# Whole-array products in the second routing's search, and fewer and earlier products of ones around the overflow loop

## The chip, the cores and the metric

The kernel runs on one core of one Trainium2 chip. The metric is the device time of one execution in microseconds (us). The engines are named as in the profile: PE is TensorE, PEld its weight loads, DVE is VectorE, ACT is ScalarE, POOL is GpSimd and SP is SyncE, which here only starts transfers.

## The reference, cut to what matters

Three steps follow each other: a causal retention attention, a first mixture of experts that routes each token to its best expert, and a second one that hands out places greedily, with a capacity of 576 tokens for each of 8 experts.

```python
x = attn(q, k, v)                       # 8 batches, 8 heads, 576 positions, 64 wide -> x [4608, 512]
skip = x @ w_skip; e1 = argmax(x @ w_gate)           # first mixture: where skip > 0
x[do] = x[do] + gate * relu(x[do] @ w1[e1]) @ w2[e1]
logits = x @ w_gate2                                 # second mixture
for idx in argsort(-logits.flatten()):               # best (token, expert) pair first
    tok, e = idx // 8, idx % 8
    if assigned[tok] < 0 and counts[e] < 576:
        assigned[tok] = e; counts[e] += 1
out[assigned == e] = relu(x[assigned == e] @ w1b[e]) @ w2b[e]
```

## The kernel before, in words

Everything is unrolled into one instruction stream per engine. The order on each engine is the order in which the Python code issues it; where the search of the second routing is woven into the matrix products, the functions `tick` and `task` decide it from counted columns, without a look at any measured time.

**Stages.** Attention runs over 36 tiles of 128 tokens. The first routing makes lists of token numbers. Then `over_blocks` (L895) opens a loop on the device that handles tokens over an expert's first 352 places; its count `nov` is computed on the chip, and all engines meet at its entrance and at its exit. Eight experts of the first mixture follow, then eight of the second. An expert's work is `layer1` (products `l1p`, L658, three passes of 128x128 weights in split fp32) and `layer2` (products `l2p`, L689), both on PE.

**The search.** The second routing needs, expert by expert, the score at which the 576th place falls. `phase(i)` (L1157) finds it by a search with base 32 in `ITS = 5` iterations; seven of the eight phases search, which makes 35 iterations. One iteration is a chain between DVE and PE:

- DVE makes the masks `M` (L179 from `digits`), PE counts with ten products into `cnt` (L1189, 128x128 weights in bf16, 32 columns moving), DVE copies to `part` in fp16 (L1191);
- PE adds up four interleaved parts into `sum` (L1195): four products whose weights are 32 columns of the identity, `eye4[:, a]`, every fourth column of `eye`, in fp16, so that the output has 32 rows; 8 columns move. DVE compares to `fl` (33 rows, the last a constant);
- PE adds the 33 rows of `fl` with a product of ones into `nfl` (L1199: weights of 33 rows and 128 columns, 8 columns moving), DVE takes the maximum (`nfs`).

Between these small products stand the large ones of `layer1` and `layer2`. After the five iterations the list of the expert's tokens is made: `idp` (L1270), then `idq` (L1279), sixteen products with 32 columns of the same `eye`, each quarter of the outputs at its own 32 columns of the array. Once a phase, the product `cct` (L1302) adds counts over all 128 rows: ones of 128x128, 8 columns moving, bf16.

**Products of ones.** `warm` (L220) issues products of ones with ones whose result nobody reads. 70 stand behind the first routing and ahead of the overflow loop (L598); ten stand behind each of the three sets of transposes `trp` (L639, called `turn`) that bring the first expert's gathered tokens into layout behind the loop (L1051). ACT copies a transposed tile to `xTH`, DVE writes the rest to `xTL`; `layer1` starts with `xTH` and needs `xTL` for its second product. Between these, the generator `gws` puts the gate weights (`gw`, `MV`) on DVE.

Of the kernel before, what the change touches and what calls it, by code (L numbers as in the profile page):

```python
# [11 lines left out]
BF16 = mybir.dt.bfloat16  # L12
F16 = mybir.dt.float16
# [8 lines left out]
N, DM, FF, E = 4608, 512, 1024, 8  # L22
NT = 36
P = 128
# [19 lines left out]
K = 32  # L44
# [118 lines left out]
def block_kernel(ctx, tc, q_c, k_c, k_r, v_r, wg, wg2, w1a, w2a, w2t, w1b, w2b, cst, dtab, out, dbg=None):  # L163
    nc = tc.nc
    V = nc.vector
# [3 lines left out]
    const = ctx.enter_context(tc.tile_pool(name="const", bufs=1))  # L169
# [8 lines left out]
    def tt(o, x, y, op):  # L178
        V.tensor_tensor(o, x, y, op)  # L179

    def ts(o, x, s1, op0, s2=None, op1=None):
        if op1 is None:
            V.tensor_scalar(o, x, s1, None, op0)
        else:
            V.tensor_scalar(o, x, s1, s2, op0, op1)

    def stt(o, x, sc, y, op0, op1):
        V.scalar_tensor_tensor(o, x, sc, y, op0, op1)  # L188

    def red(o, x, op):  # L190
        V.tensor_reduce(o, x, AX.X, op)
# [3 lines left out]
    def rt(name, shape, dt=F32, tag=None):  # L195
        return (rp if rp2[0] is None or tag else rp2[0]).tile(shape, dt, name=name, tag=tag or name)

    def last(x, n):
        return x.unsqueeze(2).to_broadcast([P, x.shape[1], n])

    def mid(x, n):
        return x.unsqueeze(1).to_broadcast([P, n, x.shape[1]])
# [4 lines left out]
    ones = const.tile([P, P], BF16, name="ones")  # L207
    iota2 = const.tile([P, P, 2], BF16, name="iota2")
    uv = const.tile([P, 2, NQ], BF16, name="uv")
    eye = const.tile([P, P], F16, name="eye")  # L210
    eye4 = eye.rearrange("p (k q) -> p q k", q=4)
    LG = const.tile([P, NT, 17], F32, name="LG")
    ident = cs[:, C_ID:C_ID + P]
    iota = cs[:, C_IOTA:C_IOTA + P]
# [5 lines left out]
    def warm(pool, tag, n):  # L220
        p = pool.tile([P, 512], F32, name="idle", tag=tag)
        for _ in range(n):
            nc.tensor.matmul(p[:, 0:P], lhsT=ones, rhs=ones, start=True, stop=True)
# [143 lines left out]
    with ExitStack() as actx:  # L367
# [4 lines left out]
        ps_x = actx.enter_context(tc.tile_pool(name="ps_x", bufs=1, space=PSUM))  # L372
# [136 lines left out]
        def tables():  # L509
            tt(um1, cs[:, C_MASK:C_MASK + P], ident, ALU.subtract)  # L510
            tt(um1, um1, ones, ALU.subtract)
            V.tensor_copy(eye, ident)
            V.tensor_copy(iota2, last(iota, 2))
            V.memset(uv, 0.0)
            V.tensor_copy(uv[:, 0, 0:NT], u_t)
            V.tensor_copy(uv[:, 1, 0:NT], v_t)
            none = rawp.tile([P, DM], F32, name="none", tag="wraw")
            nc.gpsimd.memset(none, 0.0)
            nc.gpsimd.dma_start(X[N:N + TRASH, :], none)
            nc.gpsimd.dma_start(LT[N:N + TRASH, :], none[:, 0:E])  # L520
# [29 lines left out]
        for i in range(-4, NT):  # L550
            if i in (-1, 1, 2, 3):
                c = max(i, 0) + 1
# [42 lines left out]
        route_ids()  # L595
        for _ in fuse:
            pass
        warm(ps_x, "xr", 70)  # L598

    if "LG" in dbg:  # L600
        nc.sync.dma_start(dbg["LG"], LG)
# [6 lines left out]
    ps1 = ctx.enter_context(tc.tile_pool(name="ps1", bufs=3, reuse_waits="tile", space=PSUM))  # L608
# [352 lines left out]
    kq = rt("kq", [P, K, 4], BF16)  # L961
    hl = rt("hl", [P, 2, NQ], BF16)
    z = rt("z", [P, NQ])
    fl = rt("fl", [K + 1, E], BF16)
    zb = rt("zb", [P, NQ], BF16)
    MQ = [None]

# [13 lines left out]
    def claims(a, b, src):  # L981
        n = b - a
        c = rt("c1", [P, NC, E])[:, a:b]
        red(val[:, a:b], src, ALU.max)
        tt(c, src, last(val[:, a:b], E), ALU.is_equal)
        yield
        tt(c, c, mid(w8, n), ALU.mult)
        red(mx2[:, a:b], c, ALU.max)
        yield
        stt(mx2[:, a:b], mx2[:, a:b], 1.0, un[:, a:b], ALU.add, ALU.mult)  # L990
        ts(mx2[:, a:b], mx2[:, a:b], -1.0, ALU.add)
        tt(OH[:, a:b], c, last(mx2[:, a:b], E), ALU.is_equal)
# [5 lines left out]
    def first_claims():  # L998
        V.memset(pen, 0.0)
        V.memset(vq[:, NC:NQ], 0.0)  # L1000
        V.memset(OH[:, NC:NQ], 0.0)
        V.memset(hl, 0.0)
        V.memset(fl[K:K + 1], -float(ZOFF))
        ts(kq, last(iota[:, 0:K], 4), 1.0 - ZOFF, ALU.add)
        V.tensor_copy(rm, rem)
        yield
        for _ in claims(0, NT, L2[:, 0:NT, :]):
            yield
        yield
        L2f = L2[:, 0:NT, :].rearrange("p t e -> p (t e)")  # L1010
        red(ext[:, 0:1], L2f, ALU.max)
        red(ext[:, 1:2], L2f, ALU.min)
        ts(ext[:, 1:2], ext[:, 1:2], -1.0, ALU.mult)
# [33 lines left out]
    t0 = turns(0, T1, (2,))  # L1047
    for n, j in enumerate(t0):
        next(gws)
        j()  # L1050
        warm(ps1, "l1", 10)  # L1051
    next(gws)
    for j in gathers_a(1):
        j()
# [102 lines left out]
    def phase(i):  # L1157
# [7 lines left out]
        if i < E - 1:  # L1165
            if i:
                ts(pen, opn, BIG, ALU.mult, -BIG, ALU.add)
                Lm = rt("Lm", [P, NC, E], tag="rk")
                tt(Lm, L2, mid(pen, NC), ALU.add)
                tt(rm, rem, pen, ALU.subtract)  # L1170
                yield 0.7
                for _ in claims(0, NC, Lm):
                    yield 0.7
                yield 0.7
            part = rt("part", [P, 4, E], F16)
            nf1 = rt("nf1", [P, 1])
            cnd = rt("cnd", [P, 1])
            for it in range(ITS):
                if it == 0:
                    masks(vq, lo0, inv0)  # L1180
                else:
                    masks(z, nf, ZMUL)
                while rest:
                    rest.pop(0)()
                yield MASK + LAG

                p = psm.tile([P, 4, E], F32, name="cnt", tag="sm")
                for t in range(NG):
                    nc.tensor.matmul(p.rearrange("p a e -> p (a e)"), lhsT=MQ[0][:, t].rearrange("p k a -> p (k a)"),  # L1189
                                     rhs=OH[:, 4 * t:4 * t + 4, :].rearrange("p a e -> p (a e)"), start=(t == 0), stop=(t == NG - 1))  # L1190
                V.tensor_copy(part, p)  # L1191
                yield 0.3 + LAG
                p = psm.tile([P, E], F32, name="sum", tag="sm")
                for a in range(4):
                    nc.tensor.matmul(p[0:K, :], lhsT=eye4[:, a], rhs=part[:, a, :], start=(a == 0), stop=(a == 3))  # L1195
                tt(fl[0:K], p[0:K, :], rm[0:K], ALU.is_ge)
                yield 0.3 + LAG
                p = psm.tile([P, E], F32, name="nfl", tag="sm")
                nc.tensor.matmul(p, lhsT=ones[0:K + 1, :], rhs=fl, start=True, stop=True)  # L1199
                nf = nfs[:, it:it + 1]  # L1200
                red(nf, p, ALU.max)
            ts(es, p, nf, ALU.is_equal)
            ts(nf1, nf, 1.0, ALU.add)
            tt(es, es, w8, ALU.mult)
            red(mc, es, ALU.max)
            ts(eix[:, i:i + 1], mc, -1.0, ALU.mult, 8.0, ALU.add)
            yield "expert"
            gl = rt("gl", [P, NC], BF16)
            gh = rt("gh", [P, NC], BF16)
            eo = rt("eo", [P, NC], BF16)  # L1210
            ge = rt("ge", [P, NC], BF16)
            ts(gl, zb[:, 0:NC], nf, ALU.is_ge)
            ts(gh, zb[:, 0:NC], nf1, ALU.is_ge)
            ts(eo, mx2, mc, ALU.is_equal)
            tt(ge, gh, eo, ALU.mult)
            tt(gl, gl, eo, ALU.mult)
            tt(sb[:, 1], gl, ge, ALU.subtract)
            stt(sb[:, 0], asg, mc, ge, ALU.is_equal, ALU.add)
            yield 1.8 + LAG
        else:  # L1220
            tt(es, opn, w8, ALU.mult)
            red(mc, es, ALU.max)
            ts(eix[:, i:i + 1], mc, -1.0, ALU.mult, 8.0, ALU.add)
            yield "expert"
            stt(sb[:, 0], asg, mc, un, ALU.is_equal, ALU.add)
            V.memset(sb[:, 1], 0.0)
            yield 0.5 + LAG
        p = psm.tile([P, 2, 2 * NC], F32, name="pfx", tag="sm")
# [22 lines left out]
        h1, l1 = hl[:, 0], hl[:, 1]  # L1251
# [16 lines left out]
        p = psm.tile([P, 2, 20, 4], F32, name="idp", tag="sm")  # L1268
        for t in range(NG):
            nc.tensor.matmul(p.rearrange("p j h q -> p j (h q)"), lhsT=OHl[:, t].rearrange("p k q -> p (k q)"),  # L1270
                             rhs=MV2[:, :, t].rearrange("p j h q -> p j (h q)"), start=(t == 0), stop=(t == NG - 1))
        pt2 = rt("pt2", [P, 2, 20, 4], F16)
# [3 lines left out]
        p = psm.tile([P, 10], F32, name="idq", tag="sm")  # L1276
        for a in range(4):
            for q in range(4):
                nc.tensor.matmul(p[32 * a:32 * a + 32, :], lhsT=eye4[:, q], rhs=pt2.rearrange("p j (c a) q -> p a q j c", a=4)[:, a, q],  # L1279
                                 start=(q == 0), stop=(q == 3), tile_position=(0, 32 * a), skip_group_check=True)  # L1280
        iv = rt("iv", [P, 5])
        ts(iv, p[:, 5:10], -1.0, ALU.add)
# [2 lines left out]
        if i < E - 1:  # L1285
# [15 lines left out]
            p = psm.tile([P, E], F32, name="cct", tag="sm")  # L1301
# [189 lines left out]
```

## Time and profile before

| | |
|---|---|
| median of 3 runs | 993.41 us (990.68, 993.41, 996.14) |
| the profiled execution | 988.81 us, span of the trace 987.0 us |
| busy in the span | PE 934.9 us, DVE 651.8, ACT 321.8, POOL 236.5 |
[...]

The profiled execution is one of its own, 4.6 us (0.5%) below the median of the three runs. The span runs from the first to the last instruction. A busy PE is not a PE at its peak, since products are pipelined: what one costs is read from the starts of those around it.

### The profile page before, as it was taken

What the parts mean: (1) busy time and instruction counts of PE and PEld (TensorE: products, weight loads), DVE (VectorE), ACT (ScalarE), POOL (GpSimd) and SP (SyncE); (2) the same over time, 40 slices, a digit from 0 to 9 for tenths busy, and PEclk for the clock granted to TensorE, in tenths of its full rate; (3) what the DMA queues carried; (4) which work ended last, traced back from release to release, by engine and by line L of the source; (5) the groups of instructions that cost most, each with busy time, mean ns of one, the idle gap of its engine ahead of it and who ended that gap; (6) DMA issues with size and microseconds to landing.
All of it is one profiled execution on the core that took longest, in us unless ns stands there. A gap on an engine that the chain in (4) does not pass through costs nothing.

```text
span 987.0 us, 20836 instructions
## 1 busy us (share of the span) xinstructions
PE 934.9 (95%) x8382; PEld 780.0 (79%) x8382; DVE 651.8 (66%) x1674; ACT 321.8 (33%) x610; POOL 236.5 (24%) x208
## 2 busy tenths in 40 slices
PE   7999998799999999999799999999999999999997
PEld 6788876788888888885587796887968869788886
DVE  3466585479999999865776668566685666744230
ACT  1233333134334433430143233332333323334320
POOL 2322231213544433223201203113031030330101
PEclk9999999999999999999789999999999999999999
DMA  9999994454446445410424306033060240632301
GB/s 324 361 389 361 346 376 161 153 213 157 146 168 210 134 161 176 152 53 30 149 89 154 114 22 224 23 116 141 23 224 33 100 157 12 220 117 92 107 6 43
DMA packets 57684, 153.96 MB, mean 156 GB/s; under 512 B 8464, under 2 KB 9232, under 8 KB 57328
## 3 DMA queue, kind: packets, MB, share of 16 engines
q1 hardware_dynamic: 40608, 107.50, 31.0%
q0 software_dynamic: 10496, 30.93, 9.1%
q10 hardware_dynamic: 6480, 14.16, 3.9%
q8 instruction: 67, 1.10, 0.4%
q14 instruction: 33, 0.27, 0.1%
HBM read 127.43 MB, written 25.13 MB: 155 GB/s over the span
## 4 chain that ended last, share of the span: by engine, by line
PE 67%; DVE 22%; DMA 5%; issue 4%; ACT 1%; SPq 1%; POOL 0%; POOLq 0%; ACTq 0%; DVEq 0%
PE l1p L658 28%; PE l2p L689 19%; DVE junk L756 5%; PE xTp L444 3%; PE l2p L712 3%; DVE w1L L179 3%; PE sc L418 3%; DVE w2L L179 2%; PE trp L639 2%; PE xrp L472 2%; DVE xTL L179 2%; PE xTp L441 1%; PE Sp L456 1%; DMA qT<-in_q_c_dram 1%; DMA vR<-in_v_r_dram 1%
## 5 line engine op out<-in xcount | busy, mean ns | idle before, releaser
L658 PE MATMUL l1p<-xTH,w1H 128*128 128x288 f32 (+1 forms) x768 | 243.3, 317 | 3.2 <-DVE hL L188 2.6
L658 PE MATMUL l1p<-xTL,w1H 128*128 128x288 f32 (+1 forms) x768 | 235.3, 306 | 2.0 <-DVE xTL L179 1.8
L658 PE MATMUL l1p<-xTH,w1L 128*128 128x288 f32 (+1 forms) x768 | 234.3, 305 | 0.0
L689 PE MATMUL l2p<-w2H,hH 128*128 128x512 f32 (+1 forms) x448 | 185.9, 415 | 0.0
L689 PE MATMUL l2p<-w2H,hL 128*128 128x512 f32 (+1 forms) x448 | 175.8, 392 | 0.0
L689 PE MATMUL l2p<-w2L,hH 128*128 128x512 f32 (+1 forms) x448 | 175.1, 391 | 0.0
L658 PEld LDWEIGHTS l1p<-xTH,w1H 128*128 128x128 f32 x768 | 145.4, 189 | 8.3 <-DVE hL L188 5.4
L658 PEld LDWEIGHTS l1p<-xTL,w1H 128*128 128x128 f32 x768 | 145.5, 189 | 3.4 <-DVE xTL L179 3.0
L658 PEld LDWEIGHTS l1p<-xTH,w1L 128*128 128x128 f32 x768 | 145.5, 189 | 0.0
L188 DVE SCALAR_TENSOR_TENSOR hL<-l1p,hH 128x288 fp32r<-128x288 f32 (+1 forms) x192 | 85.7, 453 | 86.6 <-ACT hH L667 84.0
L667 ACT ACTIVATE hH<-l1p 128x288 fp32r<-128x288 f32 (+1 forms) x192 | 78.5, 410 | 180.3 <-PE l1p L658 174.9
L718 POOL DMA_INDIRECT out_dram<-y,ids x40 | 43.7, 1092 | 389.4 <-DVE y L179 226.7
L689 PEld LDWEIGHTS l2p<-w2H,hH 128*128 128x128 f32 (+1 forms) x448 | 82.5, 184 | 24.2 <-issue 8.3
L756 DVE SCALAR_TENSOR_TENSOR junk<-x,wgb 128x512 f32<-128x512 f32 (+1 forms) x144 | 99.0, 688 | 3.1
L689 PEld LDWEIGHTS l2p<-w2H,hL 128*128 128x128 f32 (+1 forms) x448 | 82.4, 184 | 20.5
L689 PEld LDWEIGHTS l2p<-w2L,hH 128*128 128x128 f32 (+1 forms) x448 | 82.8, 185 | 15.0
L619 POOL DMA_INDIRECT xg<-X,ids x64 | 79.6, 1244 | 57.3 <-issue 22.9
L640 ACT ACTIVATE xTH<-trp 128x512 fp32r<-128x512 f32 (+2 forms) x64 | 35.6, 558 | 119.0 <-PE trp L639 103.4
L244 ACT ACTIVATE w1H<-wraw 128x1024 fp32r<-128x1024 f32 x64 | 65.2, 1053 | 24.4 <-DMA wraw<-in_w1b_dram 20.6
L179 DVE TENSOR_TENSOR w1L<-wraw,w1H 128x1024 fp32r<-128x1024 f32 x60 | 71.4, 1220 | 2.3 <-ACT w1H L244 1.8
L179 DVE TENSOR_TENSOR w2L<-wraw,w2H 128x1024 fp32r<-128x1024 f32 x60 | 72.7, 1213 | 0.0
L244 ACT ACTIVATE w2H<-wraw 128x1024 fp32r<-128x1024 f32 x64 | 67.4, 1054 | 15.8 <-PE l2p L689 7.3
(255 smaller groups left out, 1143.1 us busy)
## 6 DMA issues: line engine op xcount, KB each, us to landing
wraw<-in_w2a_dram SPq DMA_DIRECT2D x31, 512.0 KB
wraw<-in_w1b_dram SPq DMA_DIRECT2D x30, 512.0 KB, 3.3
wraw<-in_w2b_dram SPq DMA_DIRECT2D x30, 512.0 KB
wraw<-in_w1a_dram SPq DMA_DIRECT2D x28, 512.0 KB, 4.9
kT<-in_k_c_dram SPq DMA_DIRECT2D x36, 256.0 KB, 4.8
qT<-in_q_c_dram SPq DMA_DIRECT2D x36, 256.0 KB, 6.1
vR<-in_v_r_dram SPq DMA_DIRECT2D x36, 256.0 KB, 5.2
X<-xo ACTq DMA_DIRECT2D x36, 256.0 KB, 5.2
```

Of the source, the lines that this page charges most:

```text
L179: V.tensor_tensor(o, x, y, op)
L188: V.scalar_tensor_tensor(o, x, sc, y, op0, op1)
L244: nc.scalar.activation(h, r, AF.Copy)
L418: nc.tensor.matmul(sc[hh][c, pr, 64 * kh:P], lhsT=d["k"][r, pr, c], rhs=d["q"][r, pr, 64 * kh:P], start=True, stop=True, tile_position=(64 ...
L444: nc.tensor.matmul(xTp[o, hh, x:x + P], lhsT=d["vs"][:, 2 * pr + hh, :], rhs=d["ret"][:, hh, pr, :], start=(c == 0), stop=True, skip_group ...
L619: nc.gpsimd.indirect_dma_start(out=t[0:n, :], out_offset=None, in_=X[:, :], in_offset=bass.IndirectOffsetOnAxis(ap=ids[0:n, :], axis=0))
L640: nc.scalar.activation(h[:, :, off:off + n], p[:, :, 0:n], AF.Copy)
L658: nc.tensor.matmul(o, lhsT=wx[:, c:c + P], rhs=xx[:, k, a:b], start=(n == 0), stop=(n == 11))
L667: nc.scalar.activation(hh[0][:, f, a:b], o, AF.Relu)
L689: nc.tensor.matmul(p[0:n, :], lhsT=x[:, f, off:off + n], rhs=y[:, c:c + 512], start=(f == 0 and j == 0), stop=(f == 7 and j == 2))
L718: nc.gpsimd.indirect_dma_start(out=dst[:, :], out_offset=bass.IndirectOffsetOnAxis(ap=idx, axis=0), in_=src[0:n, :], in_offset=None)
L756: V.scalar_tensor_tensor(j[0:n], x2[0:n], 1.0, wgb[e // 4][0:n, e % 4], ALU.mult, ALU.mult, accum_out=dst[0:n, e:e + 1])
```

## The change

Three parts. (1) `strip` takes the place of `eye`: for each of the four interleaved parts, a tile of 128x128 in fp16 whose first 32 columns are those columns of the identity and whose others are zero. The four products of `sum` use all 128 columns and write all 128 rows, of which DVE still reads 32. `idq` still uses 32 columns, now adjacent ones. (2) `fl` has 128 rows, zero from row 33 on (set once in `first_claims`), and `nfl` uses ones of 128x128. (3) The products of ones ahead of the overflow loop go from 70 to 16; behind it, 16, 4 and 4 stand ahead of the three sets of transposes, where ten stood behind each.

```diff
-    eye = const.tile([P, P], F16, name="eye")
-    eye4 = eye.rearrange("p (k q) -> p q k", q=4)
+    strip = const.tile([P, 4, P], F16, name="strip")
@@ tables()
-            V.tensor_copy(eye, ident)
+            V.memset(strip, 0.0)
+            V.tensor_copy(strip[:, :, 0:32], ident.rearrange("p (k q) -> p q k", q=4))
@@ behind the first routing
-        warm(ps_x, "xr", 70)
+        warm(ps_x, "xr", 16)
@@ first_claims()
-    fl = rt("fl", [K + 1, E], BF16)
+    fl = rt("fl", [P, E], BF16)
+        V.memset(fl, 0.0)
         V.memset(fl[K:K + 1], -float(ZOFF))
@@ behind the overflow loop
     for n, j in enumerate(t0):
         next(gws)
+        warm(ps1, "l1", 16 if n == 0 else 4)
         j()
-        warm(ps1, "l1", 10)
@@ phase()
-                    nc.tensor.matmul(p[0:K, :], lhsT=eye4[:, a], rhs=part[:, a, :], start=(a == 0), stop=(a == 3))
+                    nc.tensor.matmul(p, lhsT=strip[:, a, :], rhs=part[:, a, :], start=(a == 0), stop=(a == 3))
                 tt(fl[0:K], p[0:K, :], rm[0:K], ALU.is_ge)
...
-                nc.tensor.matmul(p, lhsT=ones[0:K + 1, :], rhs=fl, start=True, stop=True)
+                nc.tensor.matmul(p, lhsT=ones, rhs=fl, start=True, stop=True)
@@ the list
-                nc.tensor.matmul(p[32 * a:32 * a + 32, :], lhsT=eye4[:, q], rhs=pt2..., ...
+                nc.tensor.matmul(p[32 * a:32 * a + 32, :], lhsT=strip[:, q, 0:32], rhs=pt2..., ...
```

PE's order inside a search iteration, between two products of layer two, before the change:

```order
L689 MATMUL l2p<-w2H_5910,hL 128x512
L1195 LDWEIGHTS eye
L1195 MATMUL sum<-part,eye 32x8
...
L689 MATMUL l2p<-w2H_5910,hH 128x512
L689 MATMUL l2p<-w2L_5911,hH 128x512
L689 MATMUL l2p<-w2H_5910,hL 128x512
L1199 LDWEIGHTS ones
L1199 MATMUL nfl<-fl,ones 128x8
```

And with the change (the lines of the changed kernel are two or three higher):

```order
L691 MATMUL l2p<-w2H_5851,hL 128x512
L1198 LDWEIGHTS strip
L1198 MATMUL sum<-part,strip 128x8
...
L691 MATMUL l2p<-w2H_5851,hH 128x512
L691 MATMUL l2p<-w2L_5852,hH 128x512
L691 MATMUL l2p<-w2H_5851,hL 128x512
L1202 LDWEIGHTS ones
L1202 MATMUL nfl<-fl,ones 128x8
```

Nothing moved here: the same number of products stands at the same places, and only the output's rows and the weights' names differ. PE's order at the exit of the overflow loop (L897 before), before the change, from the loop's branch to the first product of layer one:

```order
L897 UNCONDITIONAL_BRANCH
L639 MATMUL trp<-cs,xg 128x128 x4
L223 LDWEIGHTS ones
L223 MATMUL idle<-ones 128x128
...
L639 MATMUL trp<-cs,xg 128x96 x4
L223 LDWEIGHTS ones
L223 MATMUL idle<-ones 128x128
...
L658 MATMUL l1p<-xTH,w1H_956 128x352
```

And with the change:

```order
L899 UNCONDITIONAL_BRANCH
L224 LDWEIGHTS ones
L224 MATMUL idle<-ones 128x128
...
L641 MATMUL trp<-cs,xg 128x128 x4
L224 LDWEIGHTS ones
L224 MATMUL idle<-ones 128x128
...
L641 MATMUL trp<-cs,xg 128x96 x4
L660 MATMUL l1p<-xTH,w1H_957 128x352
```

The first set of transposes, which was PE's first work behind the loop, now has sixteen products of ones ahead of it, and none stand between the last set and layer one. On DVE, ACT, POOL and SP the order is that of before, but for DVE's two memsets.

## Rows read from the trace of the kernel before

**Rows 1.** The page's chain that ended last, by engine.

```profile
PE 67%; DVE 22%; DMA 5%; issue 4%; ACT 1%; SPq 1%; POOL 0%; POOLq 0%; ACTq 0%; DVEq 0%
```

**Rows 2.** The chain around one expert's search: start us, us, what.

```profile
599.86 0.18 DVE iv L183
...
614.99 0.61 DVE xTL L179
...
617.68 0.22 PE sum L1195 x4
...
622.95 0.26 PE cnt L1189 x10
```

**Rows 3.** PE's tile sum, all of the run: duration ns min/median/max, starts.

```profile
L1195 PE MATMUL sum<-part,eye x140: 167/174/195, 449.7 to 835.0; 128*32 128x8 f16 x140
```

**Rows 4.** PE in order of time around one nfl and one sum: start us, us.

```profile
619.49 0.40 PE L689 MATMUL l2p<-w2H,hL 128*128 128x512 f32 x1
619.81 0.18 PE L1199 MATMUL nfl<-fl,ones 33*128 33x8 bf16 x1
619.92 0.51 PE L689 MATMUL l2p<-w2H,hH 128*128 128x512 f32 x1
620.26 0.40 PE L689 MATMUL l2p<-w2L,hH 128*128 128x512 f32 x1
620.50 0.40 PE L689 MATMUL l2p<-w2H,hL 128*128 128x512 f32 x1
...
624.27 0.39 PE L689 MATMUL l2p<-w2H,hL 128*128 128x512 f32 x1
624.59 0.29 PE L1195 MATMUL sum<-part,eye 128*32 128x8 f16 x4
624.81 0.50 PE L689 MATMUL l2p<-w2H,hH 128*128 128x512 f32 x1
625.14 0.40 PE L689 MATMUL l2p<-w2L,hH 128*128 128x512 f32 x1
```

**Rows 5.** PE in order of time around one cct.

```profile
603.70 0.39 PE L689 MATMUL l2p<-w2H,hL 128*128 128x512 f32 x1
603.93 0.18 PE L1302 MATMUL cct<-ccb,ones 128*128 128x8 bf16 x1
603.97 0.48 PE L689 MATMUL l2p<-w2H,hH 128*128 128x512 f32 x1
604.29 0.39 PE L689 MATMUL l2p<-w2L,hH 128*128 128x512 f32 x1
```

**Rows 6.** The chain at the overflow loop: start us, us, what.

```profile
176.15 4.05 DMA xg<-X,ids
```

**Rows 7.** PE around the overflow loop, with idle time before a row and its releaser.

```profile
177.85 0.89 PE L223 MATMUL idle<-ones 128*128 128x128 bf16 x13 [0.52 <-issue]
181.76 1.11 PE L639 MATMUL trp<-cs,xg 128*128 128x128 f32 x4 [3.02 <-issue]
182.67 1.27 PE L223 MATMUL idle<-ones 128*128 128x128 bf16 x10
183.73 1.06 PE L639 MATMUL trp<-cs,xg 128*128 128x128 f32 x4
...
188.21 0.43 PE L658 MATMUL l1p<-xTL,w1H 128*128 128x352 f32 x1 [0.85 <-DVE xTL L179]
```

**Rows 8.** DVE behind the overflow loop, in order of time.

```profile
183.54 0.69 DVE L179 TENSOR_TENSOR xTL<-trp,xTH 128x512 fp32r<-128x512 f32 x1 [1.53 <-ACT xTH L640]
...
187.60 0.55 DVE L179 TENSOR_TENSOR xTL<-trp,xTH 128x384 fp32r<-128x384 f32 x1
```

**Rows 9.** By stretch: us, busy (instructions) of PE, PEld, DVE, ACT, POOL, then PEclk, DMA.

```profile
182.00:184.00 2.00, 2.00 (x16) 1.93 (x16) 0.47 (x2) 1.04 (x2) 1.63 (x2) 0.50 0.21 37
```

**Rows 10.** DVE in the attention, where the constants are made.

```profile
36.76 0.29 DVE L513 CAST iota<-cs 128x256 bf16<-128x256 f32 x1
```

**Rows 11.** The chain in the same stretch.

```profile
36.75 5.95 DMA vR<-in_v_r_dram
```

More of the change, by code (lines that the diff above doesn't have):

```diff
@@ L1278, in phase @@
             for q in range(4):
-                nc.tensor.matmul(p[32 * a:32 * a + 32, :], lhsT=eye4[:, q], rhs=pt2.rearrange("p j (c a) q -> p a q j c", a=4)[:, a, q],
+                nc.tensor.matmul(p[32 * a:32 * a + 32, :], lhsT=strip[:, q, 0:32], rhs=pt2.rearrange("p j (c a) q -> p a q j c", a=4)[:, a, q],
                                  start=(q == 0), stop=(q == 3), tile_position=(0, 32 * a), skip_group_check=True)
```

## Prediction

> **What bounds the kernel now.** I read the chain that ended last first: two thirds of the span are PE and 22% DVE [rows 1]. A cost on PE therefore counts only where the chain runs over PE, so the next view is the chain around one expert's search [rows 2]. It goes over DVE from the first operation on `idq`'s result (599.86) to the split of a transposed tile that ends at 615.60, and from there over PE: `sum` stands in it at 617.68 and `cnt` of the next iteration at 622.95. Walking the whole chain I find 35 `sum` and 35 `nfl`, which is every iteration of every phase; the 140 products of `sum` [rows 3] are four for each. The stretch of DVE work starts from PE's last product on the list, so time saved ahead of it lets it start earlier. Nothing in the search waits for DVE in these rows: PE is the limit there.
>
> Third I read PE in order of time. What a small product costs the large ones is not its own duration (those overlap) but the shift of the starts around it: from the start of the last large product ahead to the start of the second large product behind, less two normal steps. One step is 0.23 (603.70 to the next product's start; 620.26 to 620.50 is 0.24 after rounding) [rows 4, 5], so 0.46 for two; it is the same in all three cases below, and cancels where I subtract them.
>
> - `nfl`, 33 rows: 619.49 to 620.26 is 0.77, less 0.46: **0.31 us** [rows 4]. It starts 0.32 behind the product ahead, 0.09 late; the next follows 0.11 behind it and the one after that 0.34.
> - `sum`, four products with 32 columns: 624.27 to 625.14 is 0.87, less 0.46: **0.41 us** [rows 4]. The start is again 0.09 late, the four take 0.22, the step behind is 0.33, 0.10 too long.
> - `cct`, all rows and columns, and otherwise what `nfl` is to become (ones of 128x128, 8 columns moving, bf16): 603.70 to 604.29 is 0.59, less 0.46: **0.13 us** [rows 5]. It starts after exactly one step, and the next product follows 0.04 behind it; only the step of 0.32 after that is too long, by 0.09.
>
> So a product that uses a part of the array starts late by 0.09 and lets the next one start 0.07 later than a whole one does. What stays with the whole one is the 0.09 behind it.
>
> [...]
>
> **The change, part by part.**
>
> *`nfl` on the whole array.* The operation becomes `cct`'s: 0.31 - 0.13 = 0.18 saved, 35 times: **-6.3 us**. This is the safest term, since the same form stands in the trace. The rows of `fl` that it adds are zeros and already in place; the memset that puts them there is one of 128x8, below the 0.29 of a cast of 128x256 [rows 10], once, and I take it as nothing.
>
> *`sum` on the whole array.* No row has fp16 weights of 128 columns. The nearest is `cnt`: ten whole-array products in bf16 in 0.26 [rows 2]; with 0.04 for the first [rows 5] each further one takes (0.26 - 0.04) / 9 = 0.024. Four then cost 0.13 + 3 x 0.024 = 0.20 against 0.41 now: 0.21 saved, 35 times: **-7.35 us**. The bound on the other side comes from the only fp16 loads there are, those of `sum` itself: each further product takes (0.22 - 0.11) / 3 = 0.037 with 32 columns [rows 4]. If that is a load's time and grows with the columns, a product takes 4 x 0.037 = 0.147, and four cost 0.13 - 0.024 + 4 x 0.147 = 0.69: 0.28 lost each time, +9.8 us. I take `cnt`'s price, because it is a two-byte type with the same number of columns and rows on the same engine among the same neighbours; the type's letter is the only difference.
>
> [...]
>
> *`idq`.* Still 32 columns, adjacent now instead of every fourth. I take nothing. If its sixteen products went from 0.037 to 0.024 each, eight lists would save 1.7 us; that goes into the lower bound.
>
> *The constants.* DVE gets a memset of 128x512 in fp16, and the cast reads by strides. The cast of 128x256 next to it takes 0.29 [rows 10]; once or twice that, while the chain stands for 5.95 us on an attention load [rows 11]. The load hides it; without that cover it would cost 0.3 to 0.6 us.
>
> *Fewer products ahead of the overflow loop.* All engines wait at the loop for the third gather, which lands at 176.15 + 4.05 = 180.20 [rows 6]. PE's last product of ones ends at 177.85 + 0.89 = 178.74 [rows 7], so it was 1.5 us early and 54 products fewer bring nothing: 0. [...]
>
> *Sixteen products ahead of the first transposes.* PE is the last engine out of the loop, and its first work there was the transposes at 181.76 [rows 7]. They decide `xTH`, and DVE starts on `xTL` at 183.54 after 1.53 us of idling for it [rows 8]. From there DVE works without a break to 187.60 + 0.55 = 188.15 (three `xTL` with the gate weights between them), and layer one's second product starts at 188.21, released by the last `xTL` [rows 7, 8]. So what delays the first transposes delays layer one by as much. Ten products of ones took 183.73 - 182.67 = 1.06 at half clock [rows 7, 9]; sixteen take **+1.7 us**. [...] The products taken away between and behind the transposes saved nothing before, since DVE was the limit there; they give nothing back. Queued behind the sixteen on PE are the transposes alone, and ACT, DVE and then PE itself wait for those.
>
> **The sum.** -6.3 - 7.35 + 1.7 = -11.95, say -12.0 us. Against the profiled execution that is 988.8 - 12.0 = 976.8. That execution lies 4.6 us below the median of the three runs; the mean of the four shown is 992.3, and 992.3 - 12.0 gives **980.3 us**, which I state. A change of this kernel under 0.5%, 5 us, can hardly be told from none.
>
> **The rivals.**
>
> 1. *Fp16 loads grow with their columns* (the other side). Place: the four loads of `strip`, 35 times. The sum is -6.3 + 9.8 + 1.7 = +5.2, or **997.5**. It decides against the change where a further product takes over 0.11: there four cost 0.106 + 4 x 0.11 = 0.54, 0.13 more than now, which eats -6.3 + 1.7. For it: no fp16 load of this width in the trace. Against it: `cnt`. Chance 4%. [...]
> 2. *They grow by half as much.* Halfway between 0.024 and 0.147 is 0.085; four cost 0.106 + 4 x 0.085 = 0.45, 0.04 more than now, +1.3 in all. The sum is -6.3 + 1.3 + 1.7 = -3.3, **989**: no change that can be told. Chance 4%.
> 3. *DVE takes over in the search.* Each iteration is a ring of DVE and PE; PE's part loses 0.39. If DVE's other work (splits of weights of over 1 us in its queue) holds up half of the iterations, half the gain goes: -6.8 + 1.7 = -5.1, **987**. For it: DVE is 22% of the chain [rows 1] and owns the stretch from 599.86 to 615.60 [rows 2]. Against it: no iteration's `sum` waits for DVE there now. Chance 8%.
> 4. *The clock stays low into layer one.* With no products of ones behind the last transposes, PE idles longer ahead of layer one; if that keeps the 0.50 of rows 9 for 2 to 4 us of layer one, 1 to 2 us more: **982**. It changes the size alone. Chance 15%.
> 5. *The loop ends earlier.* If PE's arrival and not the gather had decided, 54 products at 0.89 / 13 = 0.068 would bring up to -3.7: **976.6**. Against it: 178.74 lies ahead of 180.20 [rows 6, 7]. Chance 5%.
>
> **How the numbers follow.** The main case has 64%, and with rivals 4 and 5, which only shift it, 84%. All of these are faster by over 0.5%; rival 3 stands at the edge and is split. Faster 0.88, within 0.5% 0.08, slower 0.04. For the range, the lowest value is the profiled execution with `idq`'s 1.7 or part of rival 5 taken off: 975. The highest is the median of the three runs less rival 3's 5.1: 988. Rivals 1 and 2 stay outside.
>
> **What would show it.** In the changed profile `sum` and `nfl` start one step behind the product ahead, with no 0.09; `nfl` reads like `cct`, 0.13; `sum` has 0.10 to 0.12 from its first start to the next large product, where 0.45 or more would be rival 1. From 449 to 835 us, the stretch of the 35 iterations, some 13 us are gone. Behind the loop the first transposes start 1.7 us after PE's first product of ones, at a granted clock of 0.50, and layer one's second product starts 1.7 us later against the landing of the third gather. The prediction is wrong if DVE rows appear as releasers of `sum` or `cnt` that had none, or if DVE's stretch after the list grows by what PE saved.

## The result, and the profile after

The changed kernel took 980.28 us (median of 4 runs, 978.94 to 981.93); the kernel before, timed beside it, took 992.04 (median of 4, 990.19 to 996.14). The ratio is 0.9877 with a 95% interval of 0.9838 to 0.9915: 8 to 16 us faster. 980.3 was forecast.

The profiled execution took 981.48 us; its span of 979.6 is 7.4 us shorter than that of before. That is less than the medians say, so I first ask where in the span the difference lies. The table cuts the span at events that both traces have: the last transpose of the attention (`xrp`), the first product of the eighth expert of the first mixture (the search begins in that expert's work), and the first product of the lists (`idq`) of the third and of the seventh searching phase. The last stretch holds 20 of the 35 iterations, the one ahead of it 15. Behind the seventh list the two kernels take the same time (136.7 and 136.6 us).

| us | to the last xrp | to the eighth expert | to the third list | to the seventh list |
|---|---|---|---|---|
| before | 165.55 | 254.04 | 179.83 | 250.95 |
| changed kernel | 167.46 | 258.85 | 173.48 | 243.22 |
| difference | +1.91 | **+4.81** | **-6.35** | **-7.73** |

The attention, which the change leaves alone, differs by 1.9 us between the two executions; over the profiles shown here its end lies anywhere from 164.2 to 172.7. Behind it two things are to be read: the search gives 7.73 for 20 iterations, 0.387 each (35 x 0.387 = 13.5), and something between attention and search takes 4.81. The 7.73 is read from the first products of the two lists, before and after:

```profile
599.42 0.34 PE L1279 MATMUL idq<-pt,eye 128*32 128x10 f16 x16
850.37 0.34 PE L1279 MATMUL idq<-pt,eye 128*32 128x10 f16 x16
```

```profile
599.79 0.31 PE L1282 MATMUL idq<-pt,strip 128*32 128x10 f16 x16
843.01 0.31 PE L1282 MATMUL idq<-pt,strip 128*32 128x10 f16 x16
```

**The search.** The page's chain by engine of the changed kernel; PE had 67% before and DVE 22% [rows 1]:

```profile
PE 64%; DVE 23%; DMA 6%; issue 5%; ACT 1%; POOL 0%; SPq 0%; POOLq 0%; ACTq 0%; DVEq 0%
```

The chain around the same expert's search in the changed kernel (start us, us, what), against [rows 2]:

```profile
600.19 0.18 DVE iv L183
...
615.31 0.61 DVE xTL L179
615.96 0.66 PE trp L641 x4
...
618.01 0.10 PE sum L1198 x4
...
622.97 0.26 PE cnt L1192 x10
```

The order is that of before, `sum` still stands in the chain as work of PE, and has 0.10 there where it had 0.22. DVE's stretch behind the list lasts from 600.19 to 615.92, 15.73; before it was 15.74. Over the whole run PE idles for the masks `M` ahead of `cnt` 4.8 us in six places and for `part` ahead of `sum` 0.9 us in one, the same in both kernels. PE in order of time in the changed kernel (start us, us, product, rows*columns of the weights, moving tile):

```profile
619.68 0.40 PE L691 MATMUL l2p<-w2H,hL 128*128 128x512 f32 x1
619.92 0.18 PE L1202 MATMUL nfl<-fl,ones 128*128 128x8 bf16 x1
619.96 0.47 PE L691 MATMUL l2p<-w2H,hH 128*128 128x512 f32 x1
620.27 0.39 PE L691 MATMUL l2p<-w2L,hH 128*128 128x512 f32 x1
...
624.29 0.39 PE L691 MATMUL l2p<-w2H,hL 128*128 128x512 f32 x1
624.52 0.26 PE L1198 MATMUL sum<-part,strip 128*128 128x8 f16 x4
624.64 0.48 PE L691 MATMUL l2p<-w2H,hH 128*128 128x512 f32 x1
624.96 0.39 PE L691 MATMUL l2p<-w2L,hH 128*128 128x512 f32 x1
```

`nfl` starts 0.24 behind the product ahead, which is one step, without an idle time, and the next large one 0.04 behind it: 619.68 to 620.27 is 0.59, less two steps of 0.23 is 0.13, where [rows 4] gave 0.31. `sum` starts 0.23 behind the product ahead, the next follows 0.12 later, and 624.29 to 624.96 less 0.46 is 0.21, where it was 0.41. The median over all iterations among large products is 0.12 to 0.13 for `nfl` and 0.20 to 0.21 for `sum`. A further fp16 product takes (0.114 - 0.039) / 3 = 0.025 us, with the same medians' time from `sum`'s and from `nfl`'s start to the next large product.

All 140 products of `sum` now have 128 columns. The tile in the changed kernel, against [rows 3] (duration ns min/median/max, starts): a product's own duration is hardly changed, and would have told nothing.

```profile
L1198 PE MATMUL sum<-part,strip x140: 166/166/180, 456.3 to 828.0; 128*128 128x8 f16 x140
```

**Behind the overflow loop.** The chain of the changed kernel there, against [rows 6]:

```profile
178.05 4.75 DMA xg<-X,ids
```

And PE in order of time in the changed kernel, with the idle time ahead of a row and its releaser, against [rows 7]:

```profile
184.31 1.89 PE L224 MATMUL idle<-ones 128*128 128x128 bf16 x16 [7.91 <-issue]
185.99 1.06 PE L641 MATMUL trp<-cs,xg 128*128 128x128 f32 x4
...
188.23 0.50 PE L641 MATMUL trp<-cs,xg 96*128 96x96 f32 x4
189.55 0.43 PE L660 MATMUL l1p<-xTH,w1H 128*128 128x352 f32 x1 [0.82 <-ACT xTH L642]
192.33 0.66 PE L660 MATMUL l1p<-xTL,w1H 128*128 128x352 f32 x1 [2.35 <-DVE xTL L179]
192.79 0.49 PE L660 MATMUL l1p<-xTH,w1L 128*128 128x352 f32 x1
193.08 0.49 PE L660 MATMUL l1p<-xTH,w1H 128*128 128x352 f32 x1
```

The gather lands at 182.80 and PE's first product behind the loop starts at 184.31, 1.51 later; before it was 180.20 and 181.76, 1.56 later. So the gather still sets the end of the loop. But it took 4.75 where it took 4.05, and PE's first product out of the loop starts 16.85 behind the attention's last transpose, where it started 16.21 behind. That is no chance of two executions: from the last transpose to PE's exit it is 16.85 to 17.25 in all six profiles with 16 products of ones ahead of the loop, and 16.14 to 16.53 in all eight with 70. Of the edits only the 54 products fewer stand ahead of this landing in just those six; why the gather takes longer, no run tells. The first transposes start 1.68 behind the first product of ones. Layer one's second product starts 8.02 behind PE's first product out of the loop, where it was 188.21 - 181.76 = 6.45. Its idle time ahead is 2.35, where it was 0.85, and the products behind it follow each other at 0.29. The windows of the changed kernel show why (us; busy time and instructions of PE, PEld, DVE, ACT, POOL; PEclk; DMA share; GB/s):

```profile
184.00:188.00 4.00, 3.69 (x28) 3.63 (x29) 0.74 (x2) 1.04 (x2) 2.71 (x3) 0.51 0.32 80
188.00:191.00 3.00, 1.16 (x11) 0.72 (x8) 2.86 (x9) 1.09 (x2) 0.12 (x1) 1.00 0.72 199
191.50:198.00 6.50, 5.67 (x19) 5.67 (x20) 2.10 (x6) 0.46 (x1) 0.00 (x0) 0.50 0.21 74
```

The granted clock (PEclk, a share of the full one) was 0.51 from 184 to 188, the ones and transposes, 1.00 from 188 to 191, where PE was busy for 1.16 us, and 0.50 again from 191.5 to 198. In the second profile of the changed kernel (`after_again`, below) it was 0.50 from 184 to 188 and 0.54 from 192 to 198, and layer one's first product, at 190.53, lasted 0.66 where it lasted 0.43 in the first profile. In the kernel before the same products followed each other at 0.16, and the clock was 1.00:

```profile
188.30:195.00 6.70, 6.70 (x70) 6.57 (x71) 2.29 (x7) 0.93 (x2) 0.00 (x0) 1.00 0.39 144
```

Layer one of the first expert has 96 products. From the start of its second to that of its last it took 16.46 us before and 19.07 now (this is what "the 96 products took" means below): **2.6 us** lost at the lower clock. With 8.02 - 6.45 = 1.57 that is 4.2 of the 4.81 between attention and search; the 0.64 by which PE leaves the loop later is the rest.

### The profile page after: what moved, and what is told of

It reads as the page before. It is cut to its first block, busy times and chain, and to the rows that moved or that the text cites. A ratio compares the mean times of both kernels' runs of the same rounds, so it can differ in the third digit from the quotient of the medians.

```text
span 979.6 us, 20718 instructions
## 1 busy us (share of the span) xinstructions
PE 922.7 (94%) x8322; PEld 774.5 (79%) x8322; DVE 651.1 (66%) x1676; ACT 321.9 (33%) x610; POOL 236.1 (24%) x208
## 4 chain that ended last, share of the span: by engine, by line
PE 64%; DVE 23%; DMA 6%; issue 5%; ACT 1%; POOL 0%; SPq 0%; POOLq 0%; ACTq 0%; DVEq 0%
PE l1p L660 27%; PE l2p L691 19%; DVE junk L758 5%; PE l2p L714 3%; DVE w1L L179 3%; PE xTp L445 3%; DVE w2L L179 2%; PE sc L419 2%; DMA X<-xo 2%; DVE xTL L179 2%; PE trp L641 2%; PE xrp L473 1%; PE xTp L442 1%; DMA kT<-in_k_c_dram 1%; DMA qT<-in_q_c_dram 1%
```

## Experiments

The theories: that a product on a part of the array costs 0.09 + 0.07 more among large ones, and that this is the whole gain; against it, that the loads' type or stride, or only one of the two operations, brings it. And that the new placing of the ones costs 1.7, against 4 with the time that layer one spends at the lower clock.

**The search's part alone.** The changed kernel with the products of ones as before.

```diff
-        warm(ps_x, "xr", 16)
+        warm(ps_x, "xr", 70)
...
-        warm(ps1, "l1", 16 if n == 0 else 4)
         j()
+        warm(ps1, "l1", 10)
```

> The search's products are whole as in the change; the products of ones are those of before (70 ahead of the overflow loop, ten behind each set of transposes). Theory (the switch of the array's shape is what the small products cost, and the ones behind the loop give some of it back): the stretch of the 35 iterations shrinks by 14 us as in the change, layer one's second product starts as early against the end of the loop as before, and the time is 14 us under before, 978, some 2 to 4 us under the change. Rival (the products of ones do not matter, or help): the same time as the change, 980, or above it.

978.57 us (median of 6) against 993.19 (20 runs): 0.9846 [0.9817, 0.9875]. The 20 iterations save 7.72. PE of this kernel behind the loop, and its window:

```profile
186.80 0.66 PE L641 MATMUL trp<-cs,xg 128*128 128x128 f32 x4 [3.24 <-issue]
187.29 0.98 PE L224 MATMUL idle<-ones 128*128 128x128 bf16 x10
...
192.73 0.43 PE L660 MATMUL l1p<-xTL,w1H 128*128 128x352 f32 x1 [0.89 <-DVE xTL L179]
193.00 0.32 PE L660 MATMUL l1p<-xTH,w1L 128*128 128x352 f32 x1
```

```profile
191.50:198.00 6.50, 5.61 (x63) 5.24 (x63) 3.09 (x9) 0.93 (x2) 0.00 (x0) 1.00 0.57 190
```

Layer one's second product starts 5.93 behind PE's first behind the loop, and layer one runs at 1.00: its 96 products take 16.45. So the whole gain is in the search. The forecast of 2 to 4 us under the changed kernel is not clearly met: 1.7 by the medians here, and see the repeat below.

**The ones' part alone.** The changed kernel with `sum` on 32 columns (now adjacent) and `nfl` on 33 rows.

```diff
-nc.tensor.matmul(p, lhsT=strip[:, a, :], rhs=part[:, a, :], ...
+nc.tensor.matmul(p[0:K, :], lhsT=strip[:, a, 0:K], rhs=part[:, a, :], ...
...
-nc.tensor.matmul(p, lhsT=ones, rhs=fl, ...
+nc.tensor.matmul(p, lhsT=ones[0:K + 1, :], rhs=fl[0:K + 1], ...
```

> The other half alone: the products of ones as in the change, the search's products with 32 columns and 33 rows as before (the weights still come from strip, adjacent columns). Theory: the first transposes start 1.7 us behind the end of the loop, layer one's second product 1.7 us later than before against it, 0 to 3 us more where the granted clock stays at its lower level in layer one; the search stretch is that of before; 994 to 996 against 992 for before. Rival (fewer products of ones are the gain): under 992.

995.31 (median of 12) against 993.19 (20): 1.0013 [0.999, 1.0036], no difference that can be told. In its trace the first transposes are 1.68 later behind the loop's exit, layer one's second product 8.02 behind it, and the 96 products take 19.05: the loss before the search is there, 5.27 us against the 254.04 of before. Not expected: the 20 iterations save 0.77 though `sum` still has 32 columns. It costs 0.384 among large products instead of 0.416 to 0.42, and the time from its start to the next large product is 0.185 instead of 0.22. The only edit of `sum` in this run is the columns' stride: one of its loads takes 0.093 (median of 140) with adjacent columns and took 0.117 with every fourth one, and four loads and products cost 0.035 less.

**`sum` alone, and `nfl` alone**, both with the ones as before. In the first, `nfl` has 33 rows; in the second, `sum` has 32 adjacent columns, with the edits above.

> Only sum is whole; nfl keeps its 33 rows, and the products of ones are those of before. Theory: sum costs 0.20 instead of 0.41 to 0.42 around it and nfl stays at 0.30 to 0.31, so the search stretch is 7.5 us shorter than before: 984.5. Rival (a load of 128 fp16 columns takes longer than one of 32): sum costs 0.45 or more and the time is that of before or above.

985.81 (median of 6) against 993.19: 0.9916 [0.9886, 0.9946]. `sum` costs 0.203 to 0.209, `nfl` 0.305 to 0.32; the 20 iterations save 3.95, 0.198 each.

> Only nfl is whole; sum keeps its 32 columns, and the products of ones are those of before. Theory: nfl costs 0.13 instead of 0.30 to 0.31, sum stays at 0.41, the search stretch is 6.3 us shorter: 985.7. If the gains of sum and nfl add up, this one and the one with sum alone together give that with both (14 us); if DVE or the order between them is a limit, they give more than both together.

983.97 (median of 5) against 993.19: 0.9921 [0.989, 0.9951]. `nfl` costs 0.126 to 0.133, `sum` 0.383 to 0.385; 4.38 saved, 0.219 each, of which 0.038 is the adjacent columns. The two together give 0.198 + 0.219 - 0.038 = 0.379 for an iteration, and with both it was 0.386 to 0.409 (six profiles): they add up, so nothing else becomes the limit in the search. The times alone couldn't tell: 7.4 and 9.2 us are together more than the 14.6 with both, but each of the three has an interval of some 3 us either way.

**Half of the array.** The changed kernel with 64 columns for `sum` and 65 rows for `nfl`.

```diff
+nc.tensor.matmul(p[0:64, :], lhsT=strip[:, a, 0:64], rhs=part[:, a, :], ...
...
+nc.tensor.matmul(p, lhsT=ones[0:65, :], rhs=fl[0:65], ...
```

> The change, but sum uses 64 columns and nfl 65 rows. [...] Rival (the lateness grows with the unused part): both lie between the old and the new price, sum near 0.3 and nfl near 0.2.

One run: 987.33, and 988.34 for the kernel before beside it. PE in order of time:

```profile
626.12 0.39 PE L691 MATMUL l2p<-w2H,hL 128*128 128x512 f32 x1
626.44 0.29 PE L1198 MATMUL sum<-part,strip 128*64 128x8 f16 x4
626.66 0.50 PE L691 MATMUL l2p<-w2H,hH 128*128 128x512 f32 x1
...
627.92 0.40 PE L691 MATMUL l2p<-w2H,hL 128*128 128x512 f32 x1
628.16 0.18 PE L1202 MATMUL nfl<-fl,ones 65*128 65x8 bf16 x1
628.20 0.38 PE L660 MATMUL l1p<-xTH,w1H 128*128 128x288 f32 x1
```

`sum` with 64 columns starts 0.32 behind the product ahead, 0.09 late, and costs 0.418; `nfl` with 65 rows starts on time and costs 0.126 to 0.136, like the whole one. The lateness goes by steps: 0.09 with 32 and with 64 columns, none with 128, none with 65 rows. The rest of the price is not the same at 32 and 64 columns: from its start to the next large product `sum` takes 0.218 with 64, 0.185 with 32 and 0.114 with all 128 (all adjacent). So what the whole array gains is the lateness and a shorter run of the four as well. Why 65 rows start on time where 64 columns do not, no run tells.

**Is it the part of the array, whatever the type?** `sum` with 32 adjacent columns in fp32r (`part` and the weights), `nfl` whole, the ones as before.

```diff
+    stripr = const.tile([P, 4, 32], F32R, name="stripr")
...
+            part = rt("part", [P, 4, E], F32R)
...
+nc.tensor.matmul(p[0:K, :], lhsT=stripr[:, a, :], rhs=part[:, a, :], ...
```

> nfl whole, the products of ones as before, and sum with 32 columns but in fp32r (weights and moving data), as the gate products lq are, which start one step behind the product ahead although they use 16 and 8 columns. Theory A (a part of the array costs its switch whatever the type): sum starts 0.09 late and costs 0.38 or more. Theory B (the lateness belongs to products of two-byte types, whose weight load is an instruction of its own): sum starts one step behind and costs some 0.2 to 0.3.

One run: 983.37. PE in order of time, among products of layer one whose step is 0.13:

```profile
631.47 0.29 PE L662 MATMUL l1p<-xTH,w1L 128*128 128x288 f32 x1
631.61 0.26 PE L1200 MATMUL sum<-part,stripr 128*32 128x8 f32 x4
631.73 0.38 PE L662 MATMUL l1p<-xTH,w1H 128*128 128x288 f32 x1
631.94 0.29 PE L662 MATMUL l1p<-xTL,w1H 128*128 128x288 f32 x1
```

`sum` starts 0.14 behind the product ahead, on time, and costs 0.206 to 0.212, as much as the whole one in fp16. So "a product on a part of the array starts late" is too wide: with few columns in fp32r it doesn't. The price is that of theory B; its reason, two-byte types, falls with the next two runs.

**The same question for rows**, and for fp32 that isn't fp32r. First `nfl` with 33 rows in fp32r; its `sum` takes whole 128 columns at four offsets of one strip of 224 columns (rows 32 to 127 of its output then hold numbers that nobody reads). Second, `sum` with 32 columns in plain fp32.

```diff
+    strip = const.tile([P, 7 * 32], F16, name="strip")
+    onesr = const.tile([K + 1, P], F32R, name="onesr")
...
+nc.tensor.matmul(p, lhsT=strip[:, 32 * a:32 * a + P], rhs=part[:, a, :], ...
...
+nc.tensor.matmul(p, lhsT=onesr, rhs=fl, ...
```

> sum whole, products of ones as before, and nfl with 33 rows as before the change but in fp32r (weights of ones and moving data). The strip is 224 columns wide, so that rows 32 to 127 of sum hold other numbers, which nobody reads. Theory B (a product of part of the array pays only in some types; fp32r does not pay): nfl starts one step behind and costs 0.13, and the time is that of the kernel with both whole. Theory A kept for rows (unused columns are free in fp32r, unused rows are not): nfl costs 0.30.

> As the run with sum in fp32r and 32 columns, but in plain fp32. The half tile of layer two (64 columns, plain fp32) starts 0.09 late. If it is fp32r alone that pays nothing, sum starts 0.09 late here and costs 0.4 or more (plain fp32 takes more passes over the moving data); if every product whose load belongs to the same instruction is free of it, sum starts one step behind and costs 0.2 to 0.3.

One run each: 986.8 and 996.9, with 991.85 for the kernel before (11 runs). PE in order of time in the first:

```profile
626.77 0.39 PE L693 MATMUL l2p<-w2H,hL 128*128 128x512 f32 x1
627.09 0.27 PE L1203 MATMUL nfl<-fl,onesr 33*128 33x8 f32 x1
627.29 0.40 PE L662 MATMUL l1p<-xTH,w1H 128*128 128x288 f32 x1
```

And in the second:

```profile
625.16 0.40 PE L693 MATMUL l2p<-w2H,hL 128*128 128x512 f32 x1
625.49 0.42 PE L1200 MATMUL sum<-part,stripr 128*32 128x8 f32 x8
```

33 rows in fp32r start 0.32 behind the product ahead, 0.09 late, and cost 0.39 to 0.41, more than the 0.30 that the dearer theory said; 32 columns in plain fp32 start 0.33 behind, late too, and cost 0.55 (the four products run as eight: 280 for `sum` in this trace, 140 in that of before). So fp32r is excepted for columns alone, and only it of the types tried. Why, no run tells.

**How many ones ahead of the transposes?** The changed kernel with 32 there instead of 16, and with none (16, 4 and 4 became 0, 4 and 4).

> The change with 32 instead of 16 products of ones ahead of the first set of transposes. Theory (they stand on the path from the loop's end to layer one): the first transposes start 3.2 to 3.4 us behind PE's first product of ones at the lower clock (2.6 if the clock rises half way), 1.7 us more than with 16, and layer one's second product is as much later against PE's leaving the loop, at 9.0 to 9.7 us instead of 8.0. Rival (something else, such as DVE's gate weights, sets layer one's start): it stays at 8.0.

> The change without the sixteen products ahead of the first transposes (16 ahead of the loop and four ahead of the second and third set stay). Theory: PE's first work behind the loop is the transposes again, layer one's second product comes 6.3 to 6.5 us behind PE's leaving the loop, 1.7 us earlier than in the change. The clock in layer one tells two causes apart: if the first 96 products still take 18 us or more, what is missing for the clock are the products behind the third set of transposes; if they take 16.5, it was the sixteen ahead that moved layer one into a slow stretch. 980 to 983 in the first case under 982, in the second 978 to 980.

With 32 (one run): 977.65. PE in order of time:

```profile
181.14 3.32 PE L224 MATMUL idle<-ones 128*128 128x128 bf16 x32 [7.98 <-issue]
184.29 0.61 PE L641 MATMUL trp<-cs,xg 128*128 128x128 f32 x4
...
190.25 0.43 PE L660 MATMUL l1p<-xTL,w1H 128*128 128x352 f32 x1 [3.00 <-DVE xTL L179]
```

With none: 979.59 (median of 6) against 991.85 (11), 0.9882 [0.9849, 0.9915]. PE in order of time:

```profile
182.76 1.11 PE L641 MATMUL trp<-cs,xg 128*128 128x128 f32 x4 [8.08 <-issue]
...
189.26 0.43 PE L660 MATMUL l1p<-xTL,w1H 128*128 128x352 f32 x1 [2.03 <-DVE xTL L179]
```

With 32 the transposes are 3.15 late behind the exit, and layer one's second product comes 9.11 behind it (9.0 to 9.7 forecast); with none they start at once, and it comes 6.50 behind the exit, as before the change. So the ones ahead of the transposes do delay layer one. The 96 products of layer one take 17.99 and 18.01: they lose 1.5 us with 32 ones ahead of the transposes and with none. The number of ones there is not what layer one lacks. By the expectation's rule it is then the products behind the last transposes; that is argued and not shown, since all six kernels that lose also have fewer ones ahead of the loop and around the second and third set, and no run puts back those behind the last set alone. The time with none, 979.59, lies just under the 980 to 983 that was expected for this case.

**The changed kernel against the search's part alone**, once more, on one chip.

> The changed kernel once more, beside the two that follow. Theory (search -13.7, ones +1.7 on the path and +2.6 where the clock stays low in layer one): 10 to 12 us under before. In the trace, layer one's second product 8.0 us behind PE's leaving the loop, and the first 96 products of layer one from its second on in 18 to 19 us.

> Whole products in the search with the products of ones of before, once more. Theory: 14 us under before and 2 to 4 us under the changed kernel. Rival (the ones make no difference that reaches the end): the same as the changed kernel within 1 us.

980.03 (median of 6), ratio 0.9876 [0.9845, 0.9908], and 980.80 (6), ratio 0.9878 [0.9848, 0.9908], both against 991.85 (11). The 2 to 4 us that the search's part alone was to lie under the changed kernel did not show this time: it lies 0.8 above, as the rival had it. With the earlier runs the means are 980.4 (10 runs) and 979.4 (12): 1.0 apart, with an interval of about 2 us either way. The traces put it at 4 where it arises. The stretches of the first table, of all whole versions of the search and of the kernel before with the new ones:

| us | to the eighth expert | to the third list | to the seventh list | 96 products of layer one |
|---|---|---|---|---|
| before | 254.04 | 179.83 | 250.95 | 16.46 |
| changed, first and again | 258.85, 258.32 | 173.48, 172.56 | 243.22, 242.84 | 19.07, 18.53 |
| changed, 32 ahead of the transposes | 258.90 | 172.99 | 243.17 | 17.99 |
| changed, none ahead of the transposes | 256.43 | 172.71 | 242.79 | 18.01 |
| search's part alone, first and again | 253.64, 255.21 | 175.47, 173.45 | 243.22, 242.77 | 16.45, 16.43 |
| ones' part alone | 259.31 | 178.28 | 250.19 | 19.05 |

The first column shows the cost of the ones: 4.2 on average from the search's part alone to the changed kernel, and both profiles of the former lie under both of the latter. The second column shows a scatter of 3 us in versions that do the same there, and it goes with the clock: the mean granted clock of that stretch was 0.96 in the three shortest (172.6 to 173.0), 0.95 in the two of 173.5 and 0.94 in the one of 175.5. That the new ones are behind this is a hint, no more. From the attention's last transpose to the end the changed kernel's two profiles take 812.2 and 810.3, the search's part alone 809.0 and 808.1, and the kernel before 821.5. So 2.7 of the 4.2 us reach the end in these four profiles; the times say -0.9 to 2.9, so this stays open.

## Why the prediction was right

- ***`nfl`, -6.3:*** right. 0.31 became 0.12 to 0.13, alone and together with the rest; `cct` was the right row to take it from.
- ***`sum`, -7.35:*** right in size (0.41 to 0.42 became 0.20 to 0.21; 0.21 forecast), by `cnt`'s price: 0.025 for a further fp16 product, 0.024 forecast. Rivals 1 and 2 wanted 0.147 and 0.085 and fall. The cause was a part too simple: 0.035 of the 0.21, 1.2 us of 35 iterations, is had by adjacent columns alone, a gain that the prediction weighed for `idq` only. And the prediction's rule, that a product on a part of the array starts 0.09 late, holds here for 32 and 64 columns in fp16, 32 in plain fp32, and 33 rows in bf16 and fp32r, and not for 32 columns in fp32r or 65 rows in bf16.
- ***`idq`, 0 (at most -1.7):*** 0.463 became 0.436, 0.2 us for the eight lists.
- ***Rival 3, DVE takes over:*** falls. Single gains add up (0.379, and 0.386 to 0.409 with both), and PE's idle time for `M` and `part` is that of before (4.8 and 0.9 us in the whole run).
- ***Rival 5, the loop ends earlier:*** falls. PE leaves it 1.51 behind the landing, 1.56 before. The 0 for the products ahead of the loop was not quite right either, but the other way: the gather takes 0.7 longer, and the exit comes 0.64 later.
- ***The sixteen ones, +1.7:*** right, 1.68, at a granted clock of 0.50, as forecast; they carried through to layer one's second product (1.57).
- ***Rival 4, the clock stays low into layer one:*** this happened, in every profile with the new ones (six, 1.5 to 2.6 us) and in none with the old ones (eight, all 16.4 to 16.5 us for the 96 products). The prediction gave it 15% and 1 to 2 us, and its main case said that the products taken away between and behind the transposes "give nothing back", because DVE was the limit there. DVE was (`xTL` still releases layer one), but layer one behind it lost 2.6 us (a mean granted clock of 0.55 in its first 6.5 us, 1.00 before). This is the mis-sized term: the ones cost 4.2 where they arise, not 1.7.

By the terms as measured the sum is -13.5 - 0.2 + 4.2 = -9.5, or 983 from the mean that the prediction started from; -11.8 came out by the medians. Both lie in the interval of 8 to 16 us. That the point forecast of 980.3 met the median to 0.02 is luck: the 2.5 us that its terms missed are of the size of the scatter between executions. The range of 975 to 988 holds either.

## What to carry to other kernels

A small product's price on a busy PE is the shift of the large products' starts around it, not its duration (a product of `sum` lasts 166 ns where it lasted 174, while the price of the four fell from 0.41 to 0.21 us); look first for the same operation in another form in the same trace, as `cct` was for `nfl`, and price the edit as the difference. Dummy products between a barrier and the first real work delayed that work here by about what they last (sixteen by 1.68 us at a granted clock of 0.50). Where PE idled anyhow they cost nothing (layer one's second product came 5.92 to 6.45 us behind the loop's exit in three profiles with thirty around the transposes, 6.50 with eight), and taking them away there can cost more than putting others in: layer one lost 1.5 to 2.6 us in every version with fewer of them, though which of them it lacks is not shown. When a change of 1% is made of a gain in one stage and a loss in another, compare the stages between common events: the whole span hides the loss in the scatter of stages that nobody touched.

## What the runs showed of the hardware that was not expected

- Among large products, few columns cost 0.09 of lateness in fp16 (32 and 64 columns) and in plain fp32 (32), and nothing in fp32r (32); few rows (33) cost it in bf16 and in fp32r; 65 rows cost nothing in bf16.
- Four fp16 loads of 32 adjacent columns and their products take 0.185 us to the next large product, of every fourth column 0.22; of 64 adjacent columns 0.218; of 128 columns, on the whole array, 0.114, less than either.
- The first 6.5 us from layer one's second product on ran at a mean granted clock of 0.55 to 0.74 in the six profiles with the new ones, where PE had idled 1.7 to 3.0 us just ahead of that product, and at 1.00 in the eight with the old ones, where it had idled 0.3 to 1.6. Just ahead of that the clock had been 1.00 in the changed kernel (188 to 191); in its second profile layer one's first product, 2.35 us ahead of the second, lasted 0.66 us, where in the first profile it lasted 0.43.
- The third gather landed later with 16 products of ones ahead of the overflow loop than with 70: it took 4.75 to 5.17 us in six profiles against 4.02 to 4.44 in eight. Why, no run tells.
